# Attention and mixture-of-depths kernel: 64 keys of four heads per step in 64x32 tiles

## The chip, the cores and the metric

The kernel runs on one core of one Trainium2 chip. The metric is the device time of one execution in microseconds (us). A core has a matrix engine (TensorE, PE in the profile; its weight loads are listed as PEld), a vector engine (DVE), a scalar engine (ACT), GpSimd (POOL), and SyncE (SP), whose queue issues most of the DMAs here. The engines run side by side, each in the order of its own instructions, and wait for one another by semaphores. PE writes to PSUM, which has eight banks of 128 x 512 float32; the other tiles are in SBUF.

## The reference

```
q_n, k_n = rmsnorm(q, g_q), rmsnorm(k, g_k)      # x / sqrt(mean(x*x) + 1e-6) * g
attn = softmax(q_n @ k_n.T / sqrt(64))           # q, k, v: (8, 12, 448, 64), float32
x = (attn @ v) as (8, 448, 768)                  # batch, token, 12 heads x 64
score = x @ w_gate                               # one number per token
for b in range(8):
    top = the 128 tokens of batch b with the highest score
    y = relu(x[b, top] @ w1) @ w2                # w1: 768 x 1024, w2: 1024 x 768
    out[b] = x[b]; out[b, top] += sigmoid(score[b, top]) * y
```

Everything is float32. Where the gains g_q and g_k are bounded (they are, in these inputs) no maximum is subtracted before the exponential.

## The kernel before

Twelve heads of a batch are six pairs; two pairs are a group of four heads, so there are 24 groups. One unit of the main loop (`units`, 192 of them) is 112 keys of one pair of heads against all 448 queries. `scores(u)` (line 201) makes the transposed scores of the two heads: one matmul each, 64 rows (the head's dimensions) by 112 columns (keys), the two in the upper and the lower half of PE's rows. ACT takes the exponential out of PSUM (line 218) with the key's inverse norm as its scale. `values(u)` (line 236) multiplies the probabilities by v two units later: 112 rows (keys) by 64 columns (dimensions), the two heads in the left and the right half of PE's columns, summed in PSUM over the four units of a pair. `add_probs(u)` sums the probabilities on DVE. Each float32 matmul of the program is two weight loads and two matmuls in the trace; a transpose is one of each.

`inverse_rms(n)` (line 153) prepares a group two groups ahead: ACT squares, DVE sums, POOL takes the power -0.5 (line 167), and SP sends the inverse norms of q to DRAM and back as a tile spread over all partitions (`rows`, `bc`, lines 177 and 183), by which `scale_q` (line 190) scales q. `finish_group(n)` (line 259) sums the probabilities over the keys on PE (line 264, four tiles of 112 rows x 32 columns), transposes the sums (280), and transposes and divides the result of each pair (293, 295) into the token layout x.

`mixture(b)` (line 306) runs beside the attention of the next batch, one piece per unit (each `yield` ends a piece). It stores x, gates on DVE (317), counts for every token how many score higher (336 to 367, two comparisons per quarter of the tokens), builds a 0/1 matrix `pick` (395), fetches the 128 picked rows with matmuls against it (409, and 423 for gate and row number), and does the two layers (441, 461). The product is scaled (470) and added to the output rows in DRAM by an indirect DMA of POOL (474). The mixture of the last batch has nothing beside it.

The PE instructions stand in the order in which the program is written (`manual_schedule(engines={PE})`, line 1040); the order on the other engines is found by a scheduler. One PSUM bank each serves `aux` (den, denT, x_ps) and `moe`, four serve the scores, two the products with v.

Of the kernel before, what the change touches and what calls it, by code (L numbers as in the profile page):

```python
# [26 lines left out]
def fast(  # L27
# [19 lines left out]

    nc = tc.nc

    B, NP, _, S = qT.shape  # L50
    CP = 112
    NJ = S // CP
    D = 64
    H = 2 * NP
    GH = 4
    NG = H // GH
    DM = H * D
    F = moe_w1.shape[1]
# [3 lines left out]
    NSLOT = (CAP + 127) // 128  # L62
# [3 lines left out]
    load_pool = ctx.enter_context(tc.tile_pool(name="load", bufs=3))  # L66
    norm_pool = ctx.enter_context(tc.tile_pool(name="norm", bufs=2))
    p_pool = ctx.enter_context(tc.tile_pool(name="p", bufs=5))
# [3 lines left out]
        tc.tile_pool(name="dram", bufs=3, space=bass.MemoryType.DRAM)  # L72
# [7 lines left out]
    toks, qTs, kTs, vs, rinvs, bcs, qns = {}, {}, {}, {}, {}, {}, {}  # L80
    n_groups = B * NG

    def load_tokens(n):
        b, h0 = n // NG, n % NG * GH
        for i in range(2):
            t = load_pool.tile([CP, GH, NJ, D], F32, name="tok", bufs=4)
            nc.sync.dma_start(out=t, in_=tok[b, :, i, h0 : h0 + GH])
            toks[n, i] = t

    def load_group(n):  # L90
        b, g = n // NG, n % NG
        for store, src, name in ((qTs, qT, "qT"), (kTs, kT, "kT")):
            t = load_pool.tile([128, GH // 2, S], F32, name=name, bufs=2 if name == "qT" else 3)
            nc.sync.dma_start(
                out=t, in_=src[b, g * GH // 2 : (g + 1) * GH // 2].rearrange("c p s -> p c s")
            )
            store[n] = t
        t = load_pool.tile([CP, GH, NJ, D], F32, name="v")
        nc.sync.dma_start(out=t, in_=vp[b, :, g * GH : (g + 1) * GH])
        vs[n] = t  # L100

    load_tokens(0)
    load_group(0)
    load_tokens(1)

# [6 lines left out]
    neg_half = const.tile([CP, 1], F32, name="neg_half")  # L112
    nc.vector.memset(neg_half, -0.5)
    ones = const.tile([CP, 32], F32, name="ones")
    nc.vector.memset(ones, 1.0)
# [4 lines left out]
    ident = const.tile([128, 128], F32, name="ident")  # L120
    before = const.tile([CP, NJ, NJ, CP], F32, name="before")
    slot_i = const.tile([CP, 128 * max(NSLOT, 1)], I32, name="slot_i")
    slot_f = const.tile([CP, 128 * max(NSLOT, 1)], F32, name="slot_f")
# [3 lines left out]
    def constants():  # L127
        make_identity(nc, ident)

        nc.vector.memset(before, 1.0)  # L130
        for j in range(NJ):
            nc.gpsimd.affine_select(
                out=before[:, j],
                in_=before[:, j],
                compare_op=OP.is_gt,
                fill=0.0,
                base=j,
                pattern=[[-1, NJ], [-NJ, CP]],
                channel_multiplier=NJ,
            )  # L140
        nc.gpsimd.iota(
            slot_i, pattern=[[1, 128 * max(NSLOT, 1)]], base=0, channel_multiplier=0
        )
        nc.vector.tensor_copy(out=slot_f, in_=slot_i)
        nc.gpsimd.iota(token_i, pattern=[[1, NJ]], base=0, channel_multiplier=NJ)
        nc.vector.tensor_copy(out=token_f, in_=token_i)
# [6 lines left out]
    def inverse_rms(n):  # L153

        ss = norm_pool.tile([CP, 2, GH, NJ], F32, name="ss")
        for i in range(2):
            t = toks.pop((n, i))
            sq = norm_pool.tile([CP, GH, NJ, D], F32, name="sq", bufs=1)
            nc.scalar.activation(out=sq, in_=t, func=AF.Square)  # L159
            nc.vector.tensor_reduce(out=ss[:, i], in_=sq, axis=AX.X, op=OP.add)  # L160
            yield
        rinv = norm_pool.tile([CP, 2, GH, NJ], F32, name="rinv", bufs=5)
        nc.vector.tensor_scalar(
            out=ss, in0=ss, scalar1=1.0 / D, scalar2=1e-6, op0=OP.mult, op1=OP.add
        )
        flat = "p i h j -> p (i h j)"
# [3 lines left out]
            in1=neg_half.to_broadcast([CP, 2 * GH * NJ]),  # L170
            op=OP.pow,
        )
        rinvs[n] = rinv
        yield

        rows = dram_pool.tile([GH, S], F32, name="rows")
        nc.sync.dma_start(
            out=rows.rearrange("h (p j) -> p h j", j=NJ), in_=rinv[:, 0]
        )
        bc = norm_pool.tile([128, GH // 2, S], F32, name="bc")  # L180
# [7 lines left out]
        yield  # L188

    def scale_q(g):  # L190

        n, c = divmod(g, GH // 2)
        t = norm_pool.tile([128, S], F32, name="qn", bufs=3)
        nc.vector.scalar_tensor_tensor(  # L194
            out=t, in0=qTs[n][:, c], scalar=gg, in1=bcs[n][:, c], op0=OP.mult, op1=OP.mult
        )
        qns[g] = t

    probs, sums, avs, xTs, xs = {}, {}, {}, {}, {}

    def scores(u):
        g, kc = divmod(u, NJ)
        n, c = divmod(g, GH // 2)
        p = p_pool.tile([CP, 2, S], F32, name="p")
        scs = []
# [843 lines left out]
```

## Time and profile before

| | |
|---|---|
| median of 3 runs | 799.99 us (799.12 to 800.48) |
| profiled execution | 800.58 us, of which the trace spans 798.9 us |
| PE busy | 689.0 us |
| DVE, ACT, POOL busy | 390.4, 307.0, 159.3 us |
| granted TensorE clock, mean | 0.949 of full speed |
| moved by DMA | 87.69 MB |

An engine is busy in the time that its instructions cover; PE's matmuls overlap, and their ends are modelled, so start-to-start times are the safer reading. In a row of the timeline stand the start in us, the length, the engine, the line, the operation, the tiles out<-in, shapes, and xcount; in brackets the idle time of the engine before it and what ended it.

### The profile page before, as it was taken

What the parts mean: (1) busy time and instruction counts of PE and PEld (TensorE: products, weight loads), DVE (VectorE), ACT (ScalarE), POOL (GpSimd) and SP (SyncE); (2) the same over time, 40 slices, a digit from 0 to 9 for tenths busy, and PEclk for the clock granted to TensorE, in tenths of its full rate; (3) what the DMA queues carried; (4) which work ended last, traced back from release to release, by engine and by line L of the source; (5) the groups of instructions that cost most, each with busy time, mean ns of one, the idle gap of its engine ahead of it and who ended that gap; (6) DMA issues with size and microseconds to landing.
All of it is one profiled execution on the core that took longest, in us unless ns stands there. A gap on an engine that the chain in (4) does not pass through costs nothing.

```text
span 798.9 us, 9099 instructions
## 1 busy us (share of the span) xinstructions
PE 689.0 (86%) x3520; PEld 327.0 (41%) x3520; DVE 390.4 (49%) x690; ACT 307.0 (38%) x521; POOL 159.3 (20%) x44
## 2 busy tenths in 40 slices
PE   0497798998989987999879998799999999999385
PEld 0122223553246422564226632256335633564282
DVE  3355669534673247632574426743385237622600
ACT  2355554623443245332443415433353335322000
POOL 4222653204203032021222030230420000000000
PEclk9998999998999989999899997899999999999699
DMA  5898895943543145331642406222163213000301
GB/s 161 226 373 213 198 233 139 204 111 85 167 116 93 47 114 172 104 92 49 146 152 70 116 24 170 59 70 70 32 189 78 70 34 101 1 1 1 89 1 23
DMA packets 44647, 87.69 MB, mean 110 GB/s; under 512 B 14276, under 2 KB 32708, under 8 KB 43700
## 3 DMA queue, kind: packets, MB, share of 16 engines
q1 hardware_dynamic: 43300, 83.89, 38.5%
q0 software_dynamic: 1152, 3.15, 2.6%
q8 instruction: 29, 0.48, 0.3%
q14 instruction: 22, 0.18, 0.1%
q10 hardware_dynamic: 144, 0.00, 0.0%
HBM read 72.70 MB, written 14.33 MB: 109 GB/s over the span
## 4 chain that ended last, share of the span: by engine, by line
PE 45%; issue 16%; DVE 14%; POOL 11%; DMA 7%; ACT 6%; SPq 1%; POOLq 0%; DVEq 0%; ACTq 0%
POOL rinv L167 11%; PE sc L209 11%; PE av L242 10%; PE moe_ps L461 8%; PE moe_ps L441 7%; PE moe_ps L409 5%; DMA tok<-in_tok_dram 5%; DVE ss L160 4%; ACT sq L159 3%; DVE sum L232 3%; ACT p L218 2%; DVE cmp L355 2%; DVE cmp L345 2%; PE x_ps L293 2%; DVE x L295 1%
## 5 line engine op out<-in xcount | busy, mean ns | idle before, releaser
L218 ACT ACTIVATE p<-sc,rinv 112x448 f32<-112x448 f32 x384 | 222.3, 631 | 246.5 <-PE sc L209 223.4
L209 PE MATMUL sc<-qn,kT 64*112 64x448 f32 x768 | 211.2, 615 | 50.1 <-DVE qn L194 31.5
L167 POOL TENSOR_TENSOR rinv<-ss,neg_half 112x32 f32<-112x32 f32 x24 | 142.4, 5932 | 426.3 <-ACT p L218 277.4
L242 PE MATMUL av<-p,v 112*64 112x448 f32 x768 | 194.2, 586 | 0.0
L232 DVE TENSOR_TENSOR sum<-sum,p 112x896 f32<-112x896 f32 x96 | 104.6, 1090 | 70.5 <-ACT p L218 69.9
L209 PEld LDWEIGHTS sc<-qn,kT 64*112 64x112 f32 x768 | 58.1, 180 | 132.1 <-issue 62.0
L160 DVE TENSOR_REDUCE ss<-sq 112x16 f32<-112x1024 f32 x48 | 58.5, 1219 | 98.8 <-POOL rinv L167 58.3
L242 PEld LDWEIGHTS av<-p,v 112*64 112x64 f32 x768 | 39.2, 139 | 136.4 <-issue 132.3
L441 PE MATMUL moe_ps<-xeT,w 128*128 128x128 f32 x768 | 93.9, 280 | 1.0 <-ACT hT L450 0.7
L441 PEld LDWEIGHTS moe_ps<-xeT,w 128*128 128x128 f32 x768 | 89.7, 195 | 11.3 <-issue 9.4
L461 PE MATMUL moe_ps<-w,hT 128*128 128x384 f32 x256 | 89.9, 495 | 1.4 <-DVE y L470 0.7
L159 ACT ACTIVATE sq<-tok 112x1024 f32<-112x1024 f32 x48 | 50.8, 1059 | 97.7 <-DVE ss L160 79.3
L232 DVE TENSOR_TENSOR sum<-p 112x896 f32<-112x896 f32 x48 | 52.2, 1089 | 70.5 <-ACT p L218 70.5
L461 PEld LDWEIGHTS moe_ps<-w,hT 128*128 128x128 f32 x256 | 46.2, 190 | 43.0 <-issue 14.8
L194 DVE SCALAR_TENSOR_TENSOR qn<-qT,gg,bc 128x448 f32<-128x448 f32 x48 | 32.6, 682 | 60.5 <-PE sc L209 49.4
L409 PE MATMUL moe_ps<-pick,x 112*128 112x128 f32 x384 | 48.9, 286 | 10.2 <-DVE pick L395 9.6
L409 PEld LDWEIGHTS moe_ps<-pick,x 112*128 112x128 f32 x384 | 45.9, 198 | 21.1 <-DVE pick L395 9.4
L474 POOL DMA_INDIRECT out_dram<-y,row x8 | 13.7, 1718 | 202.0 <-DVE y L470 199.7
L295 DVE TENSOR_TENSOR x<-x_ps,rden 112x512 f32<-112x512 f32 x48 | 33.0, 688 | 38.9 <-PE x_ps L293 38.6
L280 PE MATMUL denT_ps<-ident,den 128*112 128x128 f32 x96 | 19.2, 333 | 30.2 <-DVE den L274 30.0
L293 PEld LDWEIGHTS x_ps<-ident,xT 128*112 128x112 f32 x192 | 19.7, 135 | 38.2 <-DVE qn L194 9.8
L293 PE MATMUL x_ps<-ident,xT 128*112 128x128 f32 x192 | 31.6, 288 | 3.1 <-DVE x L295 2.5
(52 smaller groups left out, 259.4 us busy)
## 6 DMA issues: line engine op xcount, KB each, us to landing
tok<-in_tok_dram SPq DMA_DIRECT2D x48, 448.0 KB, 6.4
qT<-in_qT_dram SPq DMA_DIRECT2D x24, 448.0 KB, 4.9
kT<-in_kT_dram SPq DMA_DIRECT2D x24, 448.0 KB, 3.8
v<-in_vp_dram SPq DMA_DIRECT2D x24, 448.0 KB, 5.9
bc<-rows SPq DMA_DIRECT2D x48, 224.0 KB, 5.1
out_dram<-x SPq DMA_DIRECT2D x8, 1344.0 KB, 6.2
w<-in_moe_w_dram SPq DMA_DIRECT2D x2, 3072.0 KB, 17.2
rows<-rinv SPq DMA_DIRECT2D x24, 7.0 KB, 2.7
```

Source lines behind the costliest of these rows:

```text
L159: nc.scalar.activation(out=sq, in_=t, func=AF.Square)
L160: nc.vector.tensor_reduce(out=ss[:, i], in_=sq, axis=AX.X, op=OP.add)
L167: nc.gpsimd.tensor_tensor(out=rinv.rearrange(flat), in0=ss.rearrange(flat), in1=neg_half.to_broadcast([CP, 2 * GH * NJ]), op=OP.pow,)
L209: nc.tensor.matmul(out=sc[:, 0:S], lhsT=kTs[n][r, c, CP * kc : CP * (kc + 1)], rhs=qns[g][r, :], start=True, stop=True,)
L218: nc.scalar.activation(out=p[:, hh], in_=scs[hh][:, 0:S], func=AF.Exp, scale=rinvs[n][:, 1, 2 * c + hh, kc : kc + 1],)
L232: nc.vector.tensor_tensor(out=sums[g], in0=probs[u - 1] if kc == 1 else sums[g], in1=probs[u], op=OP.add)
L242: nc.tensor.matmul(out=avs[g][D * hh : D * (hh + 1), 0:S], lhsT=vs[n][:, 2 * c + hh, kc, :], rhs=probs[u][:, hh], start=(kc == 0), stop=(k ...
L293: nc.tensor.transpose(out=ps[:CP, j, :], in_=t[:, j, :], identity=ident)
L295: nc.vector.tensor_tensor(out=xs[b][:, :, col : col + 128].rearrange("p j (h d) -> p j h d", d=D), in0=ps[:CP].rearrange("p j (h d) -> p j ...
L409: nc.tensor.matmul(out=ps[:, 128 * i : 128 * i + n], lhsT=x[:, j, 128 * dc : 128 * (dc + 1)], rhs=pick[:, j, :n], start=(j == 0), stop=(j ...
L441: nc.tensor.matmul(out=ps[:, 128 * i : 128 * i + n], lhsT=w1[:, dc, 128 * (f0 + i) : 128 * (f0 + i + 1)], rhs=xeT[:, dc, :n], start=(dc == 0),
L461: nc.tensor.matmul(out=ps[:n, : DM // 2], lhsT=hT[:, fc, :n], rhs=w2[:, fc, cols], start=(fc == 0), stop=(fc == NFC - 1),)
```

## The change

All of `fast` is written anew. A group's four heads are taken together: one step is 64 keys of four heads (168 steps, seven per group). Each head's 64 keys and, for v, each head's 64 dimensions are cut in two, so that both `scores` and `values` issue eight matmuls of 64 rows x 32 columns to eight different places of the array. The loop takes two steps per turn: the scores of two steps, then the products with v of the two before.

The order on all engines is now that of the program. What is not in the two functions stands in a table `todo` of half-turns: loads, norms (`prepare`), the sums, and the gating of a batch, which is spread over ten half-turns. The mixture's two layers follow seven turns behind the gating, so that a batch's mixture lies beside the next two batches. q, k, v and the token layouts of q and k are laid out so that all 128 partitions are used (64 x 2 pairs); q is scaled in place, and the first group's norms are spread by PE instead of through DRAM.

The picked rows are no longer fetched by matmuls. The rank of a token goes as an index to four indirect DMAs of POOL, which write the rows of rank under 128 to a table in DRAM (gate and row number ride along in two more columns); SP loads the table back, PE transposes it, and the result, x added on DVE, is written over the output rows by one more indirect DMA. One comparison against a small offset takes the place of two.

```diff
-        for hh in range(2):
-            r = slice(D * hh, D * (hh + 1))
-            sc = ps_sc.tile([CP, 512], F32, name="sc")
-            nc.tensor.matmul(
-                out=sc[:, 0:S],
-                lhsT=kTs[n][r, c, CP * kc : CP * (kc + 1)],
-                rhs=qns[g][r, :],
-                start=True,
-                stop=True,
-            )
...
-        for hh in range(2):
-            nc.tensor.matmul(
-                out=avs[g][D * hh : D * (hh + 1), 0:S],
-                lhsT=vs[n][:, 2 * c + hh, kc, :],
-                rhs=probs[u][:, hh],
-                start=(kc == 0),
-                stop=(kc == NJ - 1),
-            )
...
-                        nc.tensor.matmul(
-                            out=ps[:, 128 * i : 128 * i + n],
-                            lhsT=x[:, j, 128 * dc : 128 * (dc + 1)],
-                            rhs=pick[:, j, :n],
-                            start=(j == 0),
-                            stop=(j == NJ - 1),
-                        )
...
-                compute_op=OP.add,
...
-        with tc.If(is_small > 0) as cmp, tc.manual_schedule(engines={mybir.EngineType.PE}):
+        with tc.If(is_small > 0) as cmp, tc.manual_schedule():
...
+            r = slice(D * c, D * (c + 1))
+            for i in range(NI):
+                for hh in range(2):
+                    nc.tensor.matmul(
+                        out=ps[D * hh : D * (hh + 1), D * i : D * (i + 1)],
+                        lhsT=rinv[r, hh, i : i + 1].to_broadcast([D, D]),
+                        rhs=ident[r, r],
+                        start=True,
+                        stop=True,
+                    )
...
+    def scores(u):
+        n, i = divmod(u, NI)
+        scs = [ps_sc.tile([128, 512], F32, name="sc") for _ in range(2)]
+        for c in range(2):
+            for k0 in (0, 32):
+                for hh in range(2):
+                    r = slice(D * hh, D * (hh + 1))
+                    o = D * c + k0
+                    nc.tensor.matmul(
+                        out=scs[hh][o : o + 32, 0:S],
+                        lhsT=kTs[n][r, c, D * i + k0 : D * i + k0 + 32],
+                        rhs=qTs[n][r, c, :],
+                        start=True,
+                        stop=True,
+                    )
...
+    def values(u):
+        n, i = divmod(u, NI)
+        if i == 0:
+            avs[n] = [ps_av.tile([128, 512], F32, name="av") for _ in range(2)]
+        for hh in range(2):
+            for d0 in (0, 32):
+                for c in range(2):
+                    r = slice(D * c, D * (c + 1))
+                    o = D * hh + d0
+                    nc.tensor.matmul(
+                        out=avs[n][c][o : o + 32, 0:S],
+                        lhsT=vs[n][r, hh, i, d0 : d0 + 32],
+                        rhs=probs[u][r, hh],
+                        start=(i == 0),
+                        stop=(i == NI - 1),
+                    )
...
+            nc.vector.scalar_tensor_tensor(
+                out=cmp,
+                in0=rowss[b],
+                scalar=gates[b][:, j : j + 1],
+                in1=earlier[:, j].rearrange("p a r -> p (a r)"),
+                op0=OP.subtract,
+                op1=OP.is_gt,
+                accum_out=highers[b][:, j : j + 1],
...
+    def select(b):
+        x, rank = xs.pop(b), ranks.pop(b)
+        t = dram_pool.tile([CAP, DX], F32, name="selected")
+        for j in range(NJ):
+            nc.gpsimd.indirect_dma_start(
+                out=t[:, :],
+                out_offset=bass.IndirectOffsetOnAxis(ap=rank[:, j : j + 1], axis=0),
+                in_=x[:, j, :],
+                in_offset=None,
+                bounds_check=CAP - 1,
+                oob_is_err=False,
+            )
+        slots_dram[b] = t
...
+        xe = moe_pool.tile([128, DX], F32, name="xe", bufs=2)
+        nc.sync.dma_start(out=xe[:CAP], in_=slots_dram.pop(b))
...
+                nc.tensor.transpose(
+                    out=ps[:, 128 * i : 128 * i + n],
+                    in_=xe[:n, 128 * dc : 128 * (dc + 1)],
+                    identity=ident[:n, :n],
+                )
...
+    def prepare(n, slot, step):
+        sq = {}
+        for i in range(2):
+            at(slot + i * step, lambda i=i: sq.setdefault(i, squares(n, i)))
+            at(slot + i * step + (step > 1), lambda i=i: sum_squares(n, i, sq.pop(i)))
+        at(slot + 2 * step, rows_out, n)
+        at(slot + 2 * step + 1, rows_in, n)
...
+    for n in range(1, n_groups):
+        s0 = NI * n
+        prepare(n, *((1, 1) if n == 1 else (s0 - 12, 2)))
+        at(s0 - 3, scale_q, n)
+        if n > 1:
+            at(max(s0 - 20, 0 if n == 2 else 4), load_tok, n, 0)
+            at(max(s0 - 20, 0 if n == 2 else 4), load_tok, n, 1)
+            at(s0 - 13, load_q, n)
+        at(max(s0 - 11, 0), load_k, n)
+        at(max(s0 - 11, 0), load_v, n)
...
+    first_k = {}
+    for n in range(n_groups):
+        b, g = divmod(n, NG)
+        k = (NI * (n + 1) - 1) // 2 + 1
+        t = 2 * k + 2
+        if g == 0 and b > 0:
+            t += 2
+        at(t, sum_keys, n)
+        at(t + 1, invert_sums, n)
+        at(t + 2, to_tokens, n, 0)
+        at(t + 3, to_tokens, n, 1)
+        if g == NG - 1:
+            at(t + 4, store_x, b)
+            at(t + 4, gate, b, (0, 1))
+            at(t + 5, gate, b, (2, 3))
+            at(t + 5, spread, b)
+            at(t + 6, score_rows, b)
+            at(t + 7, count, b, (0, 1))
+            at(t + 8, count, b, (2, 3))
+            at(t + 9, annotate, b)
+            at(t + 9, select, b)
+            at(t + 10, load_selected, b)
+            first_k[b] = (t + 14) // 2
+    for i in range(2):
...
+    for i in range(2):
+        sum_squares(0, i, squares(0, i))
+        if i == 0:
+            scale_q_early(0)
+    constants()
+    load_weights()
...
+    while 2 * k < units + 2 or todo or pending:
+        for u in (2 * k, 2 * k + 1):
+            if u < units:
+                scores(u)
+        late = 2 * k - 1 if (2 * k - 1) % NI == 0 else None
+        for u in (2 * k - 2, 2 * k - 1):
+            if 0 <= u < units and u != late:
+                values(u)
+                add_probs(u)
+                if u % NI == NI - 1:
+                    values_out(u // NI)
+        for fn in todo.pop(2 * k, ()):
+            fn()
+        if next(moe, moe) is moe and pending and k >= first_k[pending[0]]:
+            moe = mixture(pending.pop(0))
+            next(moe)
+        if late is not None and late < units:
+            values(late)
+            add_probs(late)
+        for fn in todo.pop(2 * k + 1, ()):
+            fn()
+        k += 1
+    for _ in moe:
+        pass
```

On PE, in the attention of a batch with a mixture beside it, this stood before (sc are scores, av products with v, L441 the first layer, L280 and L293 transposes):

```order
L423 MATMUL moe_ps<-extra,pick 128x2 x4
L209 MATMUL sc<-qn,kT 112x448 x2
L242 MATMUL av<-p,v 64x448 x2
L441 MATMUL moe_ps<-xeT,w_134 128x128 x12
L209 MATMUL sc<-qn,kT 112x448 x2
L242 MATMUL av<-p,v 64x448 x2
L264 MATMUL den_ps<-sum,ones 32x448 x4
L441 MATMUL moe_ps<-xeT,w_134 128x128 x12
```

and this stands now (L463 transposes the loaded rows, L480 is the first layer):

```order
L315 MATMUL den_ps<-sum,pick_pair 32x448 x2
L463 MATMUL moe_ps<-ident,xe 128x128 x3
L463 MATMUL xeT_ps<-ident,xe 128x128 x3
L331 MATMUL denT_ps<-ident,den 112x64 x4
L252 MATMUL sc<-qT,kT 32x448 x16
L278 MATMUL av<-p,v 32x448 x16
L345 MATMUL x_ps<-ident,xT 112x128 x4
L480 MATMUL moe_ps<-xeT,w_143 128x128 x12
L345 MATMUL x_ps<-ident,xT 112x128 x4
```

Sixteen score matmuls of two steps now stand in one run, followed by sixteen products of the same tile shape; a piece of the mixture stands between two turns instead of two units.

On SP, from the first load on, this stood before (tok are the token layouts for the norms, w the two weights):

```order
L87 DMA tok<-in_tok_dram 112x1024 x2
L177 DMA rows<-rinv 112x4x4
L94 DMA qT<-in_qT_dram 128x2x448
L94 DMA kT<-in_kT_dram 128x2x448
L183 DMA bc<-rows 64x2x448 x2
L177 DMA rows<-rinv 112x4x4
L99 DMA v<-in_vp_dram 112x1024
L87 DMA tok<-in_tok_dram 112x1024
L183 DMA bc<-rows 64x2x448 x2
L87 DMA tok<-in_tok_dram 112x1024
L149 DMA wg<-in_moe_w_gate_dram 112x768
L150 DMA w_134<-in_moe_w_dram 128x6x1024
```

and this stands now, after the loads of group 0 and the first three of group 1:

```order
L158 DMA wg<-in_moe_w_gate_dram 112x768
L159 DMA w_143<-in_moe_w_dram 128x6x1024
L160 DMA w_144<-in_moe_w_dram 128x8x768
L91 DMA kT<-in_kT_dram 128x2x448
L91 DMA v<-in_vp_dram 128x896
L91 DMA tok<-in_tok_dram 128x896 x2
L91 DMA qT<-in_qT_dram 128x2x448
L190 DMA rows<-rinv 64x2x7 x2
L91 DMA kT<-in_kT_dram 128x2x448
L91 DMA v<-in_vp_dram 128x896
L202 DMA bc<-rows 64x2x448 x2
```

The weights moved ahead of k and v of group 1, and the first pass through DRAM (rows, then bc) is that of group 1 and stands behind them.

At the end of PE's program this stood before:

```order
L242 MATMUL av<-p,v 64x448 x4
L264 MATMUL den_ps<-sum,ones 32x448 x4
L280 MATMUL denT_ps<-ident,den 112x128 x4
L293 MATMUL x_ps<-ident,xT 112x128 x8
L336 MATMUL moe_ps<-ident,spread 112x112 x4
L409 MATMUL moe_ps<-pick,x 128x128 x24
L423 MATMUL moe_ps<-extra,pick 128x2 x4
L441 MATMUL moe_ps<-xeT,w_134 128x128 x48
L461 MATMUL moe_ps<-w_135,hT 128x384 x16
```

and this stands now (the pieces between the last av and L388 belong to the batch before the last):

```order
L278 MATMUL av<-p,v 32x448 x16
L480 MATMUL moe_ps<-xeT,w_143 128x128 x12
L315 MATMUL den_ps<-sum,pick_pair 32x448 x2
L480 MATMUL moe_ps<-xeT,w_143 128x128 x12
L331 MATMUL denT_ps<-ident,den 112x64 x4
L345 MATMUL x_ps<-ident,xT 112x128 x4
L480 MATMUL moe_ps<-xeT,w_143 128x128 x12
L345 MATMUL x_ps<-ident,xT 112x128 x4
L497 MATMUL moe_ps<-w_144,hT 128x384 x4
L388 MATMUL row_ps<-ident,spread 112x112 x4
L497 MATMUL moe_ps<-w_144,hT 128x384 x12
L463 MATMUL moe_ps<-ident,xe 128x128 x3
```

Pieces of the mixture of the batch before the last, which was done by then, have moved behind the last product with v, in between the steps of the last batch's gating.

## Rows read from the trace of the kernel before

**Rows 1.** The page, its first part: busy time, share of span, instructions.

```profile
PE 689.0 (86%) x3520; PEld 327.0 (41%) x3520; DVE 390.4 (49%) x690; ACT 307.0 (38%) x521; POOL 159.3 (20%) x44
```

**Rows 2.** Busy time by stretch: length, then PE, PEld, DVE, ACT, POOL; clock; DMA.

```profile
0.00:31.50 31.50, 0.00 (x0) 0.00 (x0) 9.17 (x19) 5.51 (x5) 14.05 (x14) 1.00 0.67 169
110.00:600.00 490.00, 447.67 (x2286) 208.73 (x2288) 259.61 (x464) 201.52 (x345) 111.18 (x22) 0.95 0.42 112
738.20:798.90 60.70, 36.33 (x210) 28.70 (x208) 14.69 (x43) 2.89 (x6) 2.37 (x2) 0.84 0.17 37
```

**Rows 3.** The timeline of PE, in the attention beside no mixture.

```profile
302.52 0.97 PE L242 MATMUL av<-p,v 112*64 112x448 f32 x4
303.42 1.01 PE L209 MATMUL sc<-qn,kT 64*112 64x448 f32 x4
304.36 0.97 PE L242 MATMUL av<-p,v 112*64 112x448 f32 x4
...
310.79 0.96 PE L264 MATMUL den_ps<-sum,ones 112*32 112x448 f32 x8
311.68 0.63 PE L209 MATMUL sc<-qn,kT 64*112 64x448 f32 x2
```

**Rows 4.** PE alone between two starts in the second layer: length, busy, clock, DMA.

```profile
780.09:784.28 4.19, 4.19 (x14) 1.00 0.01 2
```

**Rows 5.** Groups of instructions: busy us, mean ns, idle before and what ended it.

```profile
L264 PE MATMUL den_ps<-sum,ones 112*32 112x448 f32 x192 | 24.7, 568 | 0.0
L280 PE MATMUL denT_ps<-ident,den 128*112 128x128 f32 x96 | 19.2, 333 | 30.2 <-DVE den L274 30.0
L293 PE MATMUL x_ps<-ident,xT 128*112 128x128 f32 x192 | 31.6, 288 | 3.1 <-DVE x L295 2.5 <-DVE rden L282 0.4
L409 PE MATMUL moe_ps<-pick,x 112*128 112x128 f32 x384 | 48.9, 286 | 10.2 <-DVE pick L395 9.6 <-ACT xeT L416 0.6
L423 PE MATMUL moe_ps<-extra,pick 112*128 112x2 f32 x64 | 8.4, 254 | 0.6 <-ACT xeT L416 0.6
L441 PE MATMUL moe_ps<-xeT,w 128*128 128x128 f32 x768 | 93.9, 280 | 1.0 <-ACT hT L450 0.7 <-DVE slot L431 0.3
L461 PE MATMUL moe_ps<-w,hT 128*128 128x384 f32 x256 | 89.9, 495 | 1.4 <-DVE y L470 0.7 <-ACT hT L450 0.7
L345 DVE TENSOR_SCALAR_CACHE_REDUCE cmp<-moe_ps,gate 112x448 f32<-112x448 f32 x32 | 21.5, 672 | 0.1
L336 PE MATMUL moe_ps<-ident,spread 112*112 112x112 f32 x32 | 6.5, 344 | 5.2 <-DVE spread L329 5.2
```

**Rows 6.** The timeline of PE where a batch's gating runs.

```profile
511.46 1.10 PE L280 MATMUL denT_ps<-ident,den 128*112 128x128 f32 x4 [5.05 <-DVE den L274]
```

**Rows 7.** The timeline of the start: first tokens, the first power, SP's issues.

```profile
4.27 0.79 SPq L87 DMA_DIRECT2D tok<-in_tok_dram  x2
...
8.28 1.28 ACT L159 ACT_TABLE_LOAD   x1 [8.28 <-DMA tok<-in_tok_dram]
...
14.53 5.45 POOL L167 TENSOR_TENSOR rinv<-ss,neg_half 112x32 f32<-112x32 f32 x1 [5.49 <-DVE extra L381]
...
49.10 0.89 SPq L177 DMA_DIRECT2D rows<-rinv  x1
...
63.38 1.23 SPq L183 DMA_DIRECT2D bc<-rows  x2
```

**Rows 8.** Two stretches of the start, as rows 2 (last column GB/s).

```profile
4.30:16.00 11.70, 0.00 (x0) 0.00 (x0) 5.03 (x10) 3.49 (x4) 4.45 (x9) 1.00 0.94 268
...
40.00:60.00 20.00, 20.00 (x98) 5.81 (x96) 10.76 (x14) 11.28 (x20) 5.42 (x1) 1.00 1.03 373
```

**Rows 9.** The timeline of the end, after the last attention.

```profile
754.87 4.77 PE L409 MATMUL moe_ps<-pick,x 112*128 112x128 f32 x24 [5.63 <-DVE pick L395]
...
765.03 7.25 PE L441 MATMUL moe_ps<-xeT,w 128*128 128x128 f32 x48 [0.25 <-DVE slot L431]
...
791.84 1.53 POOL L474 DMA_INDIRECT out_dram<-y,row  x1 [52.80 <-DVE y L470]
```

More of the change, by code (lines that the diff above doesn't have):

```diff
@@ L53, in fast @@
     D = 64
+    NI = S // D
     H = 2 * NP
@@ new lines, in add_probs, with values_out @@
+    def add_probs(u):
+        n, i = divmod(u, NI)
+        if i > 0:
+            if i == 1:
+                sums[n] = p_pool.tile([128, 2, S], F32, name="sum", bufs=2)
+            nc.vector.tensor_tensor(
+                out=sums[n], in0=probs[u - 1] if i == 1 else sums[n], in1=probs[u], op=OP.add
+            )
+            probs.pop(u - 1)
+        if i == NI - 1:
+            probs.pop(u)
+    def values_out(n):
+        for c in range(2):
+            t = norm_pool.tile([128, NJ, CP], F32, name="xT", bufs=4)
+            src = avs[n][c][:, 0:S].rearrange("d (p j) -> d j p", j=NJ)
+            if c == 0:
+                nc.scalar.copy(out=t, in_=src)
+            else:
+                nc.vector.tensor_copy(out=t, in_=src)
+            xTs[n, c] = t
+        avs.pop(n)
@@ L309, in mixture, with store_x, gate @@
+    gates, rowss, highers, ranks, slots_dram = {}, {}, {}, {}, {}
+    def store_x(b):
         nc.sync.dma_start(
-            out=out[b].rearrange("(p j) c -> p (j c)", j=NJ), in_=x.rearrange("p j c -> p (j c)")
+            out=out[b].rearrange("(p j) c -> p j c", j=NJ), in_=xs[b][:, :, 0:DM]
         )
-        if not NSLOT:
-            return
-        sc = moe_pool.tile([CP, NJ], F32, name="gate", bufs=2)
-        for j in range(NJ):
+    def gate(b, js):
+        if js[0] == 0:
+            gates[b] = moe_pool.tile([CP, NJ], F32, name="gate", bufs=2)
+        for j in js:
@@ L372, in mixture, with annotate @@
+    def annotate(b):
+        sc, x = gates.pop(b), xs[b]
+        ranks[b] = moe_pool.tile([CP, NJ], I32, name="rank", bufs=2)
+        nc.vector.tensor_copy(out=ranks[b], in_=highers.pop(b))
         parts = moe_pool.tile([CP, 2, NJ], F32, name="parts")
@@ L421, in mixture @@
-            ps = bank()
-            for j in range(NJ):
-                nc.tensor.matmul(
-                    out=ps[:n, 0:2],
-                    lhsT=pick[:, j, :n],
-                    rhs=extra[:, j, :],
-                    start=(j == 0),
-                    stop=(j == NJ - 1),
-                )
-            slot = moe_pool.tile([128, 2], F32, name="slot")
-            nc.vector.tensor_copy(out=slot[:n], in_=ps[:n, 0:2])
-            row = moe_pool.tile([128, 1], I32, name="row", bufs=2)
@@ L529, in fast @@
-    while aux:
-        drain(aux.pop(0))
-    drain(moe)
-    drain(mixture(B - 1))
+    moe, pending = iter(()), list(range(B))
+    k = 0
+    while 2 * k < units + 2 or todo or pending:
[20 more added lines that the diff above has]
+        k += 1
```

552 lines of the change are left out of this document (237 added, 315 removed).

## The prediction

> **What bounds the kernel now.** First the page's busy times [rows 1]: PE covers 689.0 of 798.9 us, DVE 390.4, ACT 307.0, POOL 159.3. Then the same by stretch [rows 2]: PE is idle to 31.5, covers 447.67 of 490 us in the middle at a mean clock of 0.95, and 36.33 of 60.70 after the last product with v. So the middle, 706.7 us from 31.5 to 738.2, is PE's, and the two ends are chains of waits.
>
> What PE does there is read from start-to-start times, since ends are modelled. A unit takes 0.94 for the scores and 0.90 for the products: 302.52 to 304.36 is 1.84 us [rows 3]. Its floor is lower. In the second layer, where PE has nothing to wait for, 4.19 us hold thirteen intervals between matmuls of 384 columns [rows 4], 0.322 each, so a matmul of 448 columns streams for 0.322 x 448/384 = 0.376 us. Each half of a unit has four matmul records, two in each of two tiles. Two rounds of 0.376 are 0.752: the two tiles run at the same time, and the remaining 0.19 and 0.15 are what it costs to go from one tile shape to the other (draining, and a first weight load that nothing covers). The key sums show more: eight records in four tiles of 32 columns, 310.79 to 311.68, take 0.89 [rows 3]. That is again two rounds and 0.14, so four tiles at a time cost no more than two.
>
> 192 units x 1.84 are 353 us. The other PE work, by its busy times [rows 5]: per group (24.7 + 19.2 + 31.6)/24 = 3.15 us for den, denT and x_ps; per batch 48.9/8 = 6.1 (pick), 8.4/8 = 1.05 (gate and row), 93.9/8 = 11.7 and 89.9/8 = 11.2 (the layers), 6.5/8 = 0.8 (score rows), 30.9. With 24 groups and seven mixtures that is 353 + 76 + 216 = 645 of the 706.7. The other 62 are waits such as the 5.05 us for DVE in the gating of a batch [rows 6], the lower clock after them, and loads at the start.
>
> **The change, part by part.** *Scores and products.* 168 steps take the place of 192 units. If the eight tiles of a step run at once, scores are two rounds and products two: 4 x 0.376 = 1.504 us, and between the two the tile shape stays the same, so that 0.19 + 0.15 per unit goes as well. 168 x 1.504 = 253 us instead of 353. Tiles side by side in rows (sc) and four in columns (den) are both shown [rows 3], the two together are not. From below nothing can pass 1.504, as every column has to stream. From above, if no more than four tiles run at once, as in den, a step is 3.0 us. I take 1.504: both directions run free, and neither the reads per partition (four streams) nor the writes (two banks) are more than in den and sc.
>
> *Key sums and transposes.* Their number per group is nearly the same; entering and leaving the new shape costs some 0.15 three times, but den now has half the matmuls in the same two rounds. I take 3.15 less 0.15.
>
> *Mixture.* Out go 6.1 and 1.05 us; in come six transposes, 1.0 us by x_ps (31.6/192 each, 0.165). The layers stay at 22.9; nine pieces per batch pay some 0.15 more each to leave the new shape. 22.9 + 1.0 + 1.3 + 0.8 = 26.0 us.
>
> *DVE, ACT, POOL.* DVE keeps its 144 sums of 896 columns and loses one of two comparisons, 21.5 us [rows 5], and gains half of the copies out of PSUM: some 380 us, over 84 turns 4.5 per turn, against PE's 3.008 + 3.0/3.5 + 26.0/10.5 = 6.34 in a turn with a mixture. Beside no mixture (turns 3.5 to 19) PE has 3.87 and DVE, without gating, 3.6: nearly even, and in-order queues on both will cost there. ACT loses 48 of 384 exponentials and stays under its 307 us. POOL's 48 powers are of 14 columns instead of 32: 2.4 us each if the 5.45 [rows 7] goes with the columns, 5.45 if it does not; even then 262 us stay covered, but a power in the start adds 3. I take 2.4. Thirty-two more indirect DMAs at 1.5 us of POOL [rows 9] are 49 us, covered.
>
> *Waits and clock.* The gating is spread over ten half-turns, and denT no longer stands behind a batch's whole comparison chain on DVE. I take 8 us (15.5 turns x 0.5) for the stretch beside no mixture and 2 per later batch, 22 in all. The ends are 8 and the 62 of now.
>
> *Start.* Group 0 gets its norms without DRAM: tokens landed at 8.28, a power of 2.4, the small matmuls, scores from about 19 and exponentials from 22 instead of 31.5. But the weights now stand ahead of k, v, rows and bc of group 1 in SP's queue. Before, a rows store issued at 49.10 behind such a queue let bc be issued only at 63.38, 14 us later [rows 7], so the queue is served in order. Ahead of rows of group 1 stand 13 loads of 0.459 MB and 6.64 MB of weights, 12.6 MB. At 268 GB/s to 16 us and 373 GB/s after [rows 8] they are through at 42; k and v of group 2 (0.92 MB) and bc come to 47.5, scaling q to 49. Group 0 is finished before 40, so PE waits and group 1 starts at 49. Without the queue it would be 37 (22 and 3.5 turns of 4.2); at 268 GB/s all along, 58.
>
> *End.* The 60.70 us of now lose pick, its matmuls and the copies, from 754.87 to 765.03, 10.2 [rows 9], and 21.5/8 = 2.7 of comparisons [rows 5]. They gain: three pieces of the mixture before, which stand in PE's order ahead of the last transposes (3 x 11.7/4 and their entries, 9.3); four indirect DMAs, of which the last is issued after 3 x 1.53 and done some 7.1 later, as long as from 791.84 to the end of the span now (11.7) [rows 2, 9]; loading the table back, about the 4 us of the first tokens (issued 4.27, there at 8.28) [rows 7]; transposes and copies, 2; and two more waits of 0.7 for a relu (ACT hT in the row of the first layer) [rows 5], as that is cut in four instead of two. 60.7 - 12.9 + 28.4 = 76.2; some of the three pieces hides behind the copies of the last group, so 75.
>
> **The sum.** From the start of group 1, 49.0; 161 steps x 1.504 = 242.1; 23 groups x 3.0 = 69.0; 6.15 mixtures (two of the seventh's nine pieces come before the last product with v) x 26.0 = 159.9; waits 22.0; end 75. That is a span of 617.0. The profiled execution was 1.7 us over its span and 0.6 over the median, so 618.1; I say 618.
>
> [...] A step has 32 matmuls and 32 weight loads in 1.504 us, 47 ns per pair. The densest rows here are eight pairs in 0.89 us [rows 3], 111 ns, and the first layer's 768 in 93.9, 122 [rows 5], and both are explained by their columns; no row shows what PE's issue can do. [...]
>
> **The rivals.** (1) *PE's issue or the eight tiles fall a little short.* If a pair takes half to two thirds of the densest 111 ns, a step takes 1.8 to 2.3 us. For it: nothing like 47 ns per pair stands in the trace. Against: four tiles with eight pairs pay no visible price. 161 x 0.3 to 0.8 adds 48 to 129: 666 to 747.
>
> (2) *Slower: at most four tiles at once.* Scores and products of each step then take turns, 3.0 us per step, on PE in the main loop. 161 x 1.504 = 241 more: 859 us, 7% slower than before. It decides from the point at which a step costs 1.504 + (800 - 618)/161 = 2.63 us. For it: the trace has no more than four tiles in flight. At the pace of the densest pairs, 111 ns, a step would be 3.55 and the time 947.
>
> (3) *DVE in its fixed order becomes the bound beside no mixture and delays PE elsewhere.* At a turn of 7.0 in place of 6.34 for 65 turns, 43 us: 661.
>
> (4) *Better than the sum:* no queue at the start (-12), waits of 8 (-14), the pieces at the end hidden (-9): 583.
>
> That the change does not do what it says would show as a step of two shapes or picked rows still fetched by PE; the orders speak against it.
>
> **How the numbers follow.** My forecast with its neighbourhood, 590 to 660, has 0.66. Rival 1 has 0.15 (660 to 750, of which 0.05 above 715), rival 3 in its upper part 0.03, rival 4 0.06, a step between 2.3 and 2.63 0.01, rival 2 0.08, no change 0.01. The range 588 to 715 leaves out 0.08 + 0.01 + 0.01 + 0.05 + 0.05 = 0.20. Differences under about 0.2% cannot be told from no change here. Faster: 0.66 + 0.15 + 0.03 + 0.06 + 0.01 = 0.91; the same 0.01; slower 0.08.
>
> **What would show it.** Right: two starts of scores 0.75 us apart without a weight load between them that waits, a step of scores and products in 1.5; the first scores near 19 us and a gap before the eighth step until about 49, ended by DVE's scaling of q, which waits for bc; no wait of 5 us before denT; the last product with v near 542 and an end of some 75 us with 15 to 20 of it between annotate and the transposes. Wrong: steps of 2 us or more with PE busy and the clock at its full level (rival 1 or 2); DVE with no idle time while PE waits for sums or q (rival 3); the start of group 1 before 40.

## The result and the profile after

| | before | after |
|---|---|---|
| median of 4 runs | 800.15 us (799.12 to 800.48) | 659.61 us (659.13 to 660.52) |
| span of the profiled execution | 798.9 us | 657.4 us |
| granted clock, mean | 0.949 | 0.928 |

The ratio is 0.8247, with a 95% interval of 0.8232 to 0.8261. The forecast was 618, so the direction and the range held, and 42 us are to be explained.

First the page's busy times of the changed kernel, which answer to [rows 1]:

```profile
PE 546.7 (83%) x6920; PEld 282.4 (43%) x6920; DVE 359.4 (55%) x588; ACT 276.8 (42%) x497; POOL 186.4 (28%) x99
```

PE lost 142 us, about what the time lost; its share of the span fell from 86 to 83%. Then the same by stretch, as in [rows 2]: the start, the main loop, and the end (stretch, length, busy time of each engine, mean granted clock, DMA share, GB/s).

```profile
46.00:580.00 534.00, 479.85 (x6430) 238.14 (x6430) 330.60 (x527) 257.20 (x463) 163.39 (x77) 0.94 0.44 142
580.00:657.40 77.40, 50.64 (x266) 36.84 (x258) 14.09 (x35) 5.44 (x13) 5.68 (x6) 0.86 0.12 40
0.00:46.00 46.00, 16.18 (x232) 7.46 (x232) 14.69 (x28) 14.19 (x21) 17.36 (x16) 0.87 0.88 323
```

In the loop PE is idle for 54 of 534 us, and the lower clock takes another 24 us of full-speed work: that is the sum, over stretches of 0.2 us, of PE's busy time multiplied by what the granted clock lacks there. (The mean of 0.94 would give 0.06 x 480 = 29, but it also counts the time in which PE stood.) The steps themselves stand in PE's timeline, beside [rows 3]:

```profile
304.24 0.43 PE L331 MATMUL denT_ps<-ident,den 64*112 64x64 f32 x4
304.61 1.74 PE L252 MATMUL sc<-qT,kT 64*32 64x448 f32 x32
306.13 1.71 PE L278 MATMUL av<-p,v 64*32 64x448 f32 x32
307.78 0.65 PE L345 MATMUL x_ps<-ident,xT 128*112 128x128 f32 x4
308.26 0.94 PE L480 MATMUL moe_ps<-xeT,w 128*128 128x128 f32 x7
```

A row of x32 holds two steps. The scores of two steps take 306.13 - 304.61 = 1.52 us and their products 1.65 where another tile shape follows (1.50 where scores follow, 67.26 to 68.76), so a step costs 1.5 to 1.6 us. The start (PE, then ACT and DVE):

```profile
16.78 4.03 PE L252 MATMUL sc<-qT,kT 64*32 64x448 f32 x32
...
39.22 2.27 PE L252 MATMUL sc<-qT,kT 64*32 64x448 f32 x16 [9.99 <-ACT p L261]
46.05 1.75 PE L252 MATMUL sc<-qT,kT 64*32 64x448 f32 x16 [4.56 <-issue]
...
37.70 0.95 ACT L167 ACTIVATE sq<-tok 128x896 f32<-128x896 f32 x1 [10.24 <-DMA tok<-in_tok_dram]
...
44.79 1.15 DVE L211 SCALAR_TENSOR_TENSOR qT<-qT,gg,bc 128x896 f32<-128x896 f32 x1 [2.70 <-DMA bc<-rows]
```

The eighth step begins at 46.05, when DVE has scaled q, and DVE waited for bc. Ten microseconds earlier PE already stood: ACT had the squares of group 2 in its order ahead of an exponential, and their tokens were loaded behind the weights. Now what PE waited for, over the whole span (us in all, times, longest):

```profile
PE moe_ps L463 <- DMA xe<-selected: 40.7, 8, 14.1
PE sc L223 <- POOL rinv L177: 14.0, 1, 14.0
PE x_ps L345 <- DVE x L347: 11.5, 10, 2.0
PE sc L252 <- ACT p L261: 11.3, 2, 10.0
PE av L278 <- ACT xT L303: 7.3, 6, 1.4
```

The largest row is a wait that the prediction placed only in the end: the table of picked rows. 14.1 of it are the last batch, the other 26.6 us stand in the loop. One of them, in the order POOL, SP, PE:

```profile
332.17 1.58 POOL L433 DMA_INDIRECT selected<-x,rank  x1 [0.81 <-DVE x L426]
335.56 0.94 POOL L433 DMA_INDIRECT selected<-x,rank  x1 [1.81 <-DMA selected<-x,rank]
338.47 1.85 POOL L433 DMA_INDIRECT selected<-x,rank  x1 [1.97 <-DMA selected<-x,rank]
342.46 2.38 POOL L433 DMA_INDIRECT selected<-x,rank  x1 [2.15 <-DMA selected<-x,rank]
...
347.46 0.33 SPq L447 DMA_DIRECT2D xe<-selected  x1
...
345.40 0.94 PE L315 MATMUL den_ps<-sum,pick_pair 128*32 128x448 f32 x4
351.17 0.90 PE L463 MATMUL moe_ps<-ident,xe 128*128 128x128 f32 x3 [4.83 <-DMA xe<-selected]
...
353.89 3.24 PE L252 MATMUL sc<-qT,kT 64*32 64x448 f32 x32
356.87 2.53 PE L278 MATMUL av<-p,v 64*32 64x448 f32 x32
```

Each indirect DMA waits until the one before it has landed, so four of them and the load back are a chain of 351.17 - 332.17 = 19 us. The written order puts the mixture's first piece two and a half turns behind `annotate`. PE stands for 4.83 us, and the next scores take 2.98 us instead of 1.52. The stretch of these scores (length, PE's busy time, granted clock, DMA) has a granted clock of 0.50, that of the scores at 304.61 one of 1.00:

```profile
353.89:356.87 2.98, 2.98 (x33) 0.50 0.94 222
```

The end is the same chain without cover:

```profile
606.57 0.94 POOL L433 DMA_INDIRECT selected<-x,rank  x1 [44.16 <-DVE x L426]
...
615.58 0.94 POOL L433 DMA_INDIRECT selected<-x,rank  x1 [2.04 <-DMA selected<-x,rank]
...
621.85 0.87 PE L463 MATMUL moe_ps<-ident,xe 128*128 128x128 f32 x3 [14.14 <-DMA xe<-selected]
```

### The profile page after: what moved, and what is told of

It is laid out like the page before. It is cut to its first block, busy times and chain, and to the rows that moved or that the text cites. A ratio compares the mean times of both kernels' runs of the same rounds, so it can differ in the third digit from the quotient of the medians.

```text
span 657.4 us, 15932 instructions
## 1 busy us (share of the span) xinstructions
PE 546.7 (83%) x6920; PEld 282.4 (43%) x6920; DVE 359.4 (55%) x588; ACT 276.8 (42%) x497; POOL 186.4 (28%) x99
## 4 chain that ended last, share of the span: by engine, by line
PE 53%; issue 21%; DMA 10%; POOL 7%; DVE 5%; ACT 3%; POOLq 0%; SPq 0%; DVEq 0%; ACTq 0%
PE sc L252 16%; PE av L278 13%; PE moe_ps L480 10%; PE moe_ps L497 7%; POOL selected L433 4%; DMA selected<-x,rank 4%; DMA xe<-selected 4%; PE x_ps L345 3%; DMA tok<-in_tok_dram 2%; POOL rinv L177 2%; ACT p L261 2%; DVE ss L173 2%; PE den_ps L315 1%; PE denT_ps L331 1%; DVE sum L291 1%
## 5 line engine op out<-in xcount | busy, mean ns | idle before, releaser
L261 ACT ACTIVATE p<-sc,rinv 128x448 f32<-128x448 f32 x336 | 186.5, 634 | 156.8 <-PE sc L252 141.2
L177 POOL TENSOR_TENSOR rinv<-ss,neg_half 128x14 f32<-128x14 f32 x48 | 136.7, 2848 | 300.6 <-DVE ss L174 280.2
L252 PE MATMUL sc<-qT,kT 64*32 64x448 f32 x2688 | 162.8, 588 | 15.9 <-ACT p L261 11.3
L278 PE MATMUL av<-p,v 64*32 64x448 f32 x2688 | 154.1, 556 | 7.3 <-ACT xT L303 7.3
L291 DVE TENSOR_TENSOR sum<-sum,p 128x896 f32<-128x896 f32 x120 | 129.3, 1077 | 4.7
L480 PEld LDWEIGHTS moe_ps<-xeT,w 128*128 128x128 f32 x768 | 90.5, 196 | 14.9 <-ACT p L261 11.0
L480 PE MATMUL moe_ps<-xeT,w 128*128 128x128 f32 x768 | 95.4, 282 | 1.5 <-ACT hT L487 1.5
L278 PEld LDWEIGHTS av<-p,v 64*32 64x32 f32 x2688 | 54.1, 111 | 90.1 <-issue 73.1
L252 PEld LDWEIGHTS sc<-qT,kT 64*32 64x32 f32 x2688 | 46.6, 111 | 83.9 <-issue 60.6
L173 DVE TENSOR_REDUCE ss<-sq 128x14 f32<-128x896 f32 x48 | 51.9, 1080 | 35.1 <-ACT sq L167 35.1
L433 POOL DMA_INDIRECT selected<-x,rank x32 | 38.7, 1210 | 95.0 <-DVE x L426 46.6
L167 ACT ACTIVATE sq<-tok 128x896 f32<-128x896 f32 x48 | 46.2, 962 | 14.8 <-DMA tok<-in_tok_dram 10.2
L345 PE MATMUL x_ps<-ident,xT 128*112 128x128 f32 x192 | 30.5, 281 | 11.9 <-DVE x L347 11.5
L463 PE MATMUL moe_ps<-ident,xe 128*128 128x128 f32 x24 | 6.5, 401 | 40.7 <-DMA xe<-selected 40.7
```

The source lines that it names most:

```text
L167: nc.scalar.activation(out=sq, in_=t, func=AF.Square, scale=scale)
L173: nc.vector.tensor_reduce(out=ss, in_=sq, axis=AX.X, op=OP.add)
L177: nc.gpsimd.tensor_tensor(out=rinv.rearrange(flat), in0=ss.rearrange(flat), in1=neg_half.to_broadcast([128, 2 * NI]), op=OP.pow,)
L252: nc.tensor.matmul(out=scs[hh][o : o + 32, 0:S], lhsT=kTs[n][r, c, D * i + k0 : D * i + k0 + 32], rhs=qTs[n][r, c, :], start=True, stop=True,)
L261: nc.scalar.activation(out=p[:, hh], in_=scs[hh][:, 0:S], func=AF.Exp, scale=rinvs[n, 1][:, hh, i : i + 1],)
L278: nc.tensor.matmul(out=avs[n][c][o : o + 32, 0:S], lhsT=vs[n][r, hh, i, d0 : d0 + 32], rhs=probs[u][r, hh], start=(i == 0), stop=(i == NI ...
```

## The experiments

The theory: the 42 us are waits in the loop, above all that for the table, and the half clock behind them. The rival: DVE, ACT or PE's own steps set the pace, and the wait only shows where PE would have stood anyway. Medians are of four runs unless the text says otherwise, intervals are of the ratio to the kernel before on the same chip (800 to 802 us).

**The mixture two turns later.**

```diff
-            first_k[b] = (t + 14) // 2
+            first_k[b] = (t + 18) // 2
```

> The mixture of a batch starts two turns later, so that the table of picked rows has two turns (some 12 us) more to come back. Theory A (the 42 us that the prediction missed are PE's waits for that table, 26.6 us in the main loop, and the half clock behind each): the waits for xe in the loop go to under 3 us, the time at the lower clock falls by 15 to 30 us, the end stays within 3 us of 77, and the whole takes 605 to 625 us. Rival B (the steps of PE or the rows of DVE are longer than the prediction took them, and the wait only stands where PE would have waited for something else): the waits move to other tiles and the time stays within 5 us of 659.6.

Measured: 630.57 us, ratio 0.7881 (0.7838 to 0.7924). The waits of this run, and its loop (its last product with v ends at 557):

```profile
PE x_ps L345 <- DVE x L347: 18.4, 11, 3.2
...
PE x_ps L345 <- DVE rden L333: 9.7, 5, 3.6
PE denT_ps L331 <- ACT den L324: 6.8, 8, 1.8
PE moe_ps L463 <- DMA xe<-selected: 5.3, 1, 5.3
```

```profile
46.00:557.00 511.00, 470.06 (x6403) 231.41 (x6404) 330.08 (x528) 255.26 (x461) 164.98 (x77) 0.96 0.46 150
```

The wait for the table is gone from the loop (the 5.3 are in the end), and 29 us with it, some 24 of them in the loop: the theory holds. But the time stays above 605 to 625, as the waits for DVE before x_ps grew from 11.8 (11.5 and 0.3 for rden) to 28.1 us. The end is 72 instead of 77 us, which was not expected: PE waits 5.3 us there for the last table instead of 14.1, as more of the mixture of the batch before now stands ahead of it.

**The weights behind the loads of the next groups.**

```diff
-    load_weights()
+    at(8, load_weights)
```

> The loads of the weights are issued behind those of the next groups in the queue instead of ahead of them. Theory A (the start is set by the queue: tok of group 2 lands late and holds ACT, then rows and bc of group 1 come late): the wait of 9.99 us for p and that of 4.56 before scale_q go, step 7 begins near 36 to 38 us instead of 46.05, and the time is 8 to 12 us lower, 648 to 652. Rival B (PE is bound later by the picked rows, whose place follows the fixed order, and what the start gains is lost there): under 3 us.

Measured: 660.81 us, ratio 0.8266 (0.8223 to 0.8309): no gain. From PE's and DVE's timelines:

```profile
40.57 1.75 PE L252 MATMUL sc<-qT,kT 64*32 64x448 f32 x16 [8.78 <-issue]
...
78.81 1.10 PE L345 MATMUL x_ps<-ident,xT 128*112 128x128 f32 x4 [7.76 <-DVE x L347]
...
77.00 1.15 DVE L211 SCALAR_TENSOR_TENSOR qT<-qT,gg,bc 128x896 f32<-128x896 f32 x1 [7.07 <-DMA bc<-rows]
```

The eighth step began at 40.57, 5.5 us earlier, and not at 36 to 38. Before 77.00 DVE waited 7.07 us for the bc of a later group, which now stood behind the weights, and PE waited 7.76 us behind it. The queue sets the start, but the block only moved the wait. Rival B had the right size by another cause.

**Tiles of 64x64.**

```diff
-            for k0 in (0, 32):
+            for k0 in (0,):
...
-                        out=scs[hh][o : o + 32, 0:S],
+                        out=scs[hh][o : o + 64, 0:S],
...
```

(and `values` in the same way)

> Scores and products of a step in 64x64 tiles, four tiles at once and 16 pairs of weight load and matmul each, instead of eight tiles of 64x32 and 32 pairs. Theory A (a step costs its four rounds through the array, 1.504 us, and issue is free): a step stays at 1.50 to 1.55 us and the time within 4 us of 659.6. Rival B (PE's issue of 47 ns per pair is at its limit, so half the instructions save time): a step falls under 1.45 and 161 steps give 10 us or more. Rival C (a 64x64 tile takes its columns more slowly or blocks a neighbour): a step of 2 us or more, 740 or above.

Measured: 657.12 us, ratio 0.8207 (0.8182 to 0.8232), 2.5 us less, with an interval that just touches that of the changed kernel.

```profile
303.97 1.73 PE L252 MATMUL sc<-qT,kT 64*64 64x448 f32 x16
305.52 1.68 PE L278 MATMUL av<-p,v 64*64 64x448 f32 x16
307.13 0.65 PE L345 MATMUL x_ps<-ident,xT 128*112 128x128 f32 x4
```

Half the instructions, and 1.55 and 1.61 us for what took 1.52 and 1.65. Here the columns set the pace, not the number of instructions.

**The order fixed on PE alone.**

```diff
-        ... tc.manual_schedule():
+        ... tc.manual_schedule(engines={mybir.EngineType.PE}):
```

> The written order holds for PE alone; on the other engines the program's scheduler sets the order again. Theory A (what costs is PE's own order, which puts the mixture at a fixed turn; the other engines have slack of 45% and more): the time stays within 10 us of 659.6, and the waits for the table of picked rows stay at 3 to 5 us per batch. Rival B (the order on ACT, DVE and POOL is itself worth much, since a pieces of gating that stands ahead of an exponential or a sum stops PE): 20 us or more slower, with waits for p or av in many steps.

Measured: 794.28 us, ratio 0.9908 (0.9879 to 0.9937). Theory A falls by 125 us. What PE waited for:

```profile
PE x_ps L345 <- DVE x L347: 68.8, 15, 10.8
PE av L278 <- ACT xT L303: 39.0, 10, 9.6
PE denT_ps L331 <- ACT den L324: 18.0, 6, 6.0
PE sc L252 <- DVE qT L211: 17.7, 1, 17.7
```

Four short instructions of DVE and ACT, each with PE right behind it, came late by up to 17.7 us, on engines that were busy for 363.0 and 278.6 of 791.9 us. Idle time of an engine does not say that its next result comes when it is wanted.

**The kernel before with the order fixed on all engines** (the opposite edit, in the kernel before):

> The kernel before with one line changed: its written order holds on all engines and not on PE alone. With the changed kernel the same line was worth 794 against 660 us. Theory A (the order alone helps only where PE has time to give back; before, PE was busy for 448 of 490 us in the middle, and its order there was already the written one): 770 to 830 us. Rival B (the written order on the other engines is worth as much here, so that the gain is the order's and not the tiles'): 700 us or less. A written order that was never followed on DVE and ACT may also cost: above 830.

Measured: 798.04 us (10 runs), ratio 0.9954 (0.9935 to 0.9972): theory A. The order alone is worth 4 us, the rest of the change without it 7, and both together 141.

**Picked rows by matmuls again.**

```diff
-            nc.gpsimd.indirect_dma_start(
-                out=t[:, :],
+            nc.vector.tensor_scalar(
+                out=pick[:, j],
...
-                nc.tensor.transpose(
+                for j in range(NJ):
+                    nc.tensor.matmul(
```

> One part undone: the rows are again picked on PE by matmuls with a comparison table, and the results are added to DRAM at the end; no table of picked rows goes through DRAM. Theory A (the indirect rows cost PE their waits, 40.7 us in all and the half clock behind each, and saved it some 6 us of matmuls per batch): the waits for xe go, PE gains 8 x 6 us of matmuls and DVE 8 x 2.5 us of comparisons; the two nearly cancel, 645 to 670 us, with an end 5 to 10 us shorter than 77. Rival B (the picked rows are what made the kernel faster, beside the shape of the tiles): 690 us or more.

Measured: 637.95 us, ratio 0.7955 (0.7924 to 0.7987), 22 us faster than the changed kernel and below the 645 to 670 of theory A. Its loop, to the last product with v:

```profile
46.00:565.00 519.00, 496.50 (x6756) 268.63 (x6756) 337.26 (x556) 255.45 (x462) 142.89 (x49) 0.99 0.44 137
```

PE has 17 us more busy time than in the changed kernel and yet its loop is 15 us shorter: idle 22.5 instead of 54.2 us, clock 0.99 instead of 0.94. So the indirect rows, as placed, cost more in waits than they saved in matmuls. Placed two turns later they win by 7 us (630.57) over matmuls at the old place; matmuls two turns later were not tried.

**The weights in fourteen pieces**, one per half turn from slot 12 ("the run before this one" below is the block at slot 8):

```diff
...
-    load_weights()
+    at(10, load_weights)
+    for c in range(NDC):
+        at(12 + c, load_w1, c)
+    for c in range(NFC):
+        at(12 + NDC + c, load_w2, c)
```

> The weights are loaded in fourteen pieces, one per half turn from slot 12 on, instead of 6.64 MB at once (ahead of group 1 in the changed kernel, in one block from slot 8 in the run before this one). Theory A (the start is set by the loads that stand in one queue; in one block they only move the wait from 46 us to 71 us, where bc of group 3 ended a wait of 7.75): step 7 begins near 40 us, no wait over 3 us stands between 40 and 100, and the time is 5 to 9 us lower than 659.6, 650 to 655. Rival B (the fixed order gives the time back at the picked rows, whatever the start): within 2 us of 659.6.

Measured: 656.64 us, ratio 0.8201 (0.8166 to 0.8237), between theory A's 650 to 655 and rival B. The eighth step begins at 41.29, and from there to 98 us PE's longest wait is 1.59 us; the profiled execution kept all of it (its span is 651.9, 5.5 us less), the medians differ by 3.0, with intervals that overlap. The size stays open between these.

**The mixture's addition later in DVE's order**, on top of two turns later: half a turn, behind `sum_squares` and `scale_q`.

```diff
-            nc.vector.scalar_tensor_tensor(
+            def add_slots(a=a, cols=cols, ps=ps):
+                nc.vector.scalar_tensor_tensor(
...
+            yield add_slots
...
+        if callable(last):
+            last()
```

> The mixture two turns later as in the first run, and in DVE's order the addition of the mixture to the rows (two per batch) stands half a turn later, behind the squares' sums and the scaling of q. In the first run PE still waited 18.4 us for DVE before the second x_ps and 9.7 for rden, and DVE before them stood 5.1 us at this addition, waiting for PE. Theory A (DVE in its fixed order is the next limit, by what stands behind a wait): these waits fall by half or more and the time is 5 to 12 us lower than the first run's 630.6. Rival B (DVE has the same work in the same turn, so the wait moves to q or to the sums): within 3 us of 630.6.

Measured: 622.08 us, ratio 0.7767 (0.7736 to 0.7797), 8.5 us less, as theory A had it. DVE's timeline with two turns later alone, and then with this:

```profile
340.80 0.62 DVE L506 SCALAR_TENSOR_TENSOR xe<-moe_ps,xe 128x384 f32<-128x384 f32 x1 [5.13 <-PE moe_ps L497]
```

```profile
337.91 0.26 DVE L333 RECIPROCAL rden<-denT_ps 112x16 f32<-112x16 f32 x1 [1.70 <-PE denT_ps L331]
338.09 0.52 DVE L508 SCALAR_TENSOR_TENSOR xe<-moe_ps,xe 128x384 f32<-128x384 f32 x1
```

DVE no longer stands for the mixture with a scale of q behind it. Yet PE's waits before x_ps hardly fell (17.1 and 7.1 us): theory A had the size, and not the place. The loop is 9 us shorter, 5.2 of it in PE's idle time (40.9 to 35.7 us) and 3.8 in its busy time (470.1 to 466.3).

**Five of six key sums left out**, on top of that. This kernel leaves out most of the sums by which the softmax divides; it serves to ask what they cost.

```diff
-        if i > 0:
+        if i == 1:
```

> The last run (mixture two turns later, its addition later in DVE's order) with five of the six additions of each group's probabilities left out, so that the key sums hold two of seven steps: 120 instructions of 1.08 us, 130 us, less on DVE. Theory A (the waits for DVE that are left, 17.1 us before x_ps and 7.1 for rden, come from what stands ahead of those rows in DVE's order): they fall to under 8 us together, the time at half clock with them, and the time is 15 to 30 us lower than 622.1, 592 to 607. Rival B (they come from PE's single buffer for x_ps and denT, a round trip over DVE that has its length whatever else DVE does): within 5 us of 622.1.

Measured: 610.60 us, ratio 0.7609 (0.7560 to 0.7658), 11.5 us less, between the two.

```profile
PE x_ps L345 <- DVE x L347: 9.5, 11, 1.1
PE x_ps L345 <- DVE rden L333: 7.1, 4, 4.5
```

A third of DVE's work is gone, and only 7.6 of the 24.2 us. What is left may be a round trip: one PSUM bank serves den, denT, x_ps and half of the transposes, so that PE has to wait until the tile before it is read. That this bank is the cause was not tried.

**All that won, together**: two turns later, the later addition, 64x64 tiles, weights in pieces.

> What won so far, together: the mixture two turns later, its addition later in DVE's order, 64x64 tiles, and the weights in fourteen pieces. If the gains of 29.1, 8.5, 2.5 and 3.0 us add up, 616.5; if what the start gains is lost again at the next wait, 620; if the waits for DVE eat part of it, 622.

Measured: 616.54 us, ratio 0.7691 (0.7665 to 0.7716): the gains add up, and the rivals' 620 and 622 lie outside the interval (614.7 to 618.8 us). This is the fastest version that leaves nothing out, 6.5% below the changed kernel.

**The same with the mixture one turn later instead of two**, `(t + 16) // 2`:

> The same with the mixture one turn later instead of two. Theory A (the chain from annotate to the table is some 19 us, and one turn of 6 to 7 us more than the changed kernel's 15 covers it but for the first us): waits for xe under 1.5 us per batch in the loop, and the end not longer; within 4 us of the kernel with two turns. Rival B (the chain gets longer as PE gets faster): 5 to 15 us more.

Measured: 630.89 us, ratio 0.7863 (0.7818 to 0.7909), 14 us more: rival B's size, though the waits for xe in the loop went as theory A had it (the 7.5 us below are in the end). PE's idle time in the loop is 46.5 instead of 34.9 us. PE's waits show a new place:

```profile
PE x_ps L349 <- DVE rden L337: 12.0, 4, 5.3
PE xeT_ps L467 <- DVE row L477: 9.8, 7, 3.0
PE sc L256 <- issue: 9.2, 1, 9.2
PE moe_ps L467 <- DMA xe<-selected: 7.5, 1, 7.5
```

In the loop the table is there for the first transposes, but the second ones and rden, which share a bank and DVE's order with `row`, come late (9.8 and 12.0 us, the latter 7.4 with two turns), while the waits for x fell from 17.5 to 4.4. Covering a wait is not enough where the place of a piece also decides what stands around it.

## Why the prediction was right, and where it missed

*Steps.* Right: 1.504 forecast, 1.5 to 1.6 in the trace, all eight tiles at once. Rivals 1 and 2 fall by that row. 32 pairs of load and matmul in 1.52 us are 47 ns each. The price of another tile shape behind a step, 0.15, came too (1.65 against 1.50 us); what it is made of no run takes apart.

*Sums and transposes of a group.* Taken at 3.0 us; the rows show den at about 0.94 (345.40 in the timeline), denT 0.37 and twice 0.48 for x_ps, 2.3 us. Over 23 groups that is 16 us too much: the busy times of [rows 5] count modelled ends and stretches at half clock, which starts at full clock leave out, and the four transposes of denT have 64 columns now instead of 128, where the prediction took their cost as nearly the same. The forecast of all work in the loop was 242.1 + 69.0 + 159.9 = 471 us. Measured, 480 us busy less 24 for the clock is 456. The run with two turns later gives 470 less 17, by the same sum, 453.

*Waits and clock.* This is the step that failed, a term mis-sized: 22 us forecast, 54 + 24 = 78 measured. Of the 54, 26.6 are for the table, to which the prediction gave nothing in the loop; all the other waits together are some 27. The prediction reckoned the chain of the picked rows in the end (15.7 us from the first indirect DMA to the transposes; 621.85 - 606.57 = 15.3 came, by luck: from the first issue to the fourth it took 9.0 instead of 4.6 us, from there to the transposes 6.3 instead of 11.1), but not against the two and a half turns of some 6.3 us that the table `todo` gives it in the loop. It called the indirect DMAs covered because POOL was free; POOL was, PE was not. 56 us too few here and 15 too many in the work are the 41 us by which the loop is longer (534.3 instead of 493). Rival 3, waits for DVE, named 661 and so came near the measured 659.6 by luck: its mechanism ruled only after the table was out of the way.

*Start.* 49 forecast, 46.05 measured, ended by scaling and bc as said; the first scores came at 16.78 instead of 19. That ACT stands behind tokens of a later group was not seen. Without the block the gain is 5 us at step 7, not 12 (rival 4). In that run k and v of group 2 still stand ahead of bc in the queue; that they cost the rest was not tried.

*End.* 75 forecast, 657.4 - 580.3 = 77.1 measured, and its parts fit too: 26.3 to the first indirect DMA, 15.3 for the chain and 35.6 behind it, against 23.3, 15.7 and 37.3 in the prediction's terms.

*The order on all engines.* The prediction gave it no price of its own, and all else rests on it: without it the change is worth 7 us.

## What to carry to other kernels

A chain that is priced at the end of a kernel must also be laid against its cover at every earlier place where it runs: count the turns between the producer and the first consumer. Moving work from the bound engine to DMAs gained here only where the consumer stood far enough behind: 637.95 us with matmuls, 659.61 with DMAs, 630.57 with DMAs and the mixture two turns later. A wait on PE can cost more than its length: behind the 4.83 us above the granted clock was 0.50, and the next scores took 1.46 us longer. When a step becomes shorter, what stands ahead of each short result on the other engines must be in order first: with the order on PE alone DVE and ACT were busy for 363.0 and 278.6 of 791.9 us, and PE still waited for them up to 17.7 us at a time.

## What the runs showed that was not expected

- The forecast took it, but no row of the kernel before had shown it: eight tiles of 64x32 stream side by side in both directions of the array (32 matmuls of 448 columns in 1.52 us), and issue keeps up at 47 ns per pair. 64x64 tiles with half the instructions take the same time (1.55 against 1.52 us for two steps of scores).
- A wait of 4.83 us is followed by slower steps: scores at 2.98 instead of 1.52 us at a granted clock of 0.50, products at 2.47 instead of 1.65 at 0.66. In the run with matmuls for the picked rows PE's idle time in the loop is 22.5 us and the clock 0.99 of full speed; with the order on PE alone the clock is 0.877 over the span.
- The four indirect DMAs into one table follow one another at 2.7 to 4.0 us, as each waits for the landing of the one before it (so the trace has it for 23 of the 24 that follow another, 45.3 us of POOL's waiting in all), though they write different rows.
